# Masked blocks between the halves of a linear attention: one FP32 product instead of three FP32R products, with another order on VectorE

## The chip, the cores and the metric

The kernel runs on one core of a Trainium2 chip. The metric is the device time of one execution in microseconds (us). The program is launched once; the median of three runs before the change is 1372.36 us (1371.91 to 1373.18).

The engines are named as in the profile: PE is TensorE (matmul), PEld its loads of the stationary operand, DVE is VectorE, ACT is ScalarE, POOL is GpSimd, SP is SyncE, which here issues most of the DMA transfers.

## What is computed

Two layers of the same kind, each an attention half A and a mixing half B, on x of 2048 tokens by 512 features, all in float32:

```
x = x + A(layernorm(x));  x = x + B(layernorm(x))      # twice

A: qkv = x @ wqkv, 32 heads of 16
   phi(t) = where(t > 0, t + 1, exp(t)) + 1e-6
   kv[h] = phi(k)[h].T @ v[h];   z[h] = sum over tokens of phi(k)[h]
   o = (phi(q) @ kv) / (phi(q) . z + 1e-6);   A = o @ wo

B: z = gelu(x @ w_in);  z1, z2 = halves of z, z2 layer-normalised
   g = w_sp @ z2 + b_sp;   B = (z1 * g) @ w_out
```

The kernel does not compute v. It uses that kv = phi(k).T @ (x @ wv) can be had from G = x.T @ phi(k), summed over all tokens, since wv.T @ G is the transpose of kv. Of the 512x512 product only the 16x16 blocks on the diagonal belong to a head. The kernel computes the four 128x128 diagonal blocks and multiplies each by a mask that keeps the head blocks. These are the masked blocks. They are then multiplied by wo into W2, so that each query tile needs a single product with W2.

## The kernel before

**Precision.** A matmul here normally runs on FP32R operands, a reduced form of float32. To keep float32 precision, an operand is split into a high part (an ACT copy that rounds to FP32R, `high`, line 105) and a low part (the remainder, a DVE subtraction, `low`, line 108, or on POOL, line 113). `mm3` (lines 117 to 121) makes three matmuls of one product: high x high, high x low, low x high. So every 128-deep step of a product is three matmuls, and every operand costs one ACT and one DVE instruction.

**Buffers.** SBUF is cut into slots: 22 pages of 128x512 (`pg`), 6 quads of 128x2048 (`qd`), 4 bigs (`bg`), 16 larger token tiles (`z`); PSUM into 8 banks. `Slots.get` and `put` hand them out in order of release. A tile that gets a slot waits for the last readers of the slot's former tile. The program is recorded in the order of the calls, with one queue per engine; there is no scheduler, so that the order of the Python statements is the order on each engine.

**First half, `P1.run`** (line 496). Over 16 token tiles of 128, in iterations s = 1 to 17: load, layer norm, transposition through DRAM, the K projection and phi(k), the Q projection and phi(q), and `Gmm`, the accumulation of G into four PSUM banks (12 matmuls per 128 tokens). At the end of every iteration stand side pieces: the weights for later (wv, wo, win2) are loaded into pages by SP (`fetch`) and split into quads or bigs (`piece`). wv takes two quads, high and low, from iterations 1 to 4. The Q projection of the last 6 tiles is put off (`late`, `late_phi`), as PE work that covers the transition.

**`transition`** (line 541) joins the halves:

- z, the sum of phi(k), is split (lines 545, 546) and summed over partitions by a product with ones (555, 556); ACT copies it to `zbc` (559).
- G is copied out of its four banks and split into two quads (550 to 553).
- POOL multiplies phi(q) of a tile with zbc (`a`, line 631).
- `late_phi` finishes a put-off query tile: ACT lines 363 and 364, DVE line 365.
- DVE sums zbc per head into `zeps` (566 to 568); `a2_den` gets the reciprocal of a tile's denominator (643 to 645).
- The masked blocks q = 0 to 3 (572 to 578): each is 4 steps of `mm3`, 12 matmuls of 128x128, 48 in a layer. DVE multiplies each by the mask (577). Then they are split in two pairs (580, 581).
- `a2_mul` (652) applies the denominator to a query tile; for tile 0 an ACT copy (276) puts it in order for four PE transposes (`b`, line 257).
- One put-off Q projection (587), 12 matmuls of 512 columns, stands on PE between the masked blocks and their use.
- W2: four products of a split block with the split wo (592), each split into W2 on ACT and DVE (593); after the second one come the transposes of query tile 0 (596).

**Second half.** `P2.run` takes the query tiles through W2, and goes on to half B; `P4.run` does the token mixing and the output.

Of the kernel before, what the change touches and what calls it, by code (L numbers as in the profile page):

```python
# [11 lines left out]
F32R = mybir.dt.float32r  # L12
AF = mybir.ActivationFunctionType
OP = mybir.AluOpType

P = 128
# [41 lines left out]
def mixer_kernel(ctx: ExitStack, tc: tile.TileContext, x_in, wqkv, wo_d, win1_d, win2_d, wsp_d, bsp_d, wout_d,  # L58
                 ident_d, mask_d, out_d):
    nc = tc.nc  # L60
# [8 lines left out]
    quads = Slots(main, "qd", 6)  # L69
# [34 lines left out]
    def high(h, src):  # L104
        nc.scalar.activation(h, src, AF.Copy)  # L105

    def low(l, src, h):
        nc.vector.tensor_sub(l, src, h.bitcast(F32))  # L108

    def split(h, l, src, pool=False):  # L110
        high(h, src)
        if pool:
            nc.gpsimd.tensor_tensor(l, src, h.bitcast(F32), op=OP.subtract)
        else:
            low(l, src, h)

    def mm3(out, a, b, start, stop):
        (ah, al), (bh, bl) = a, b
        nc.tensor.matmul(out, ah, bh, start=start, stop=False)  # L119
        nc.tensor.matmul(out, ah, bl, start=False, stop=False)  # L120
        nc.tensor.matmul(out, al, bh, start=False, stop=stop)  # L121

    class Weight:


        def __init__(self, slots, shape, pieces, turned=False):
            self.slots, self.shape, self.pieces, self.turned = slots, shape, pieces, turned
            self.h = self.l = None
            self.raw = deque()
            self.n_load = self.n_split = 0  # L130
# [82 lines left out]
    def w_square(src, off, turned=False):  # L213
        return Weight(quads, [P, 4, 512], [src[c * P:(c + 1) * P, off:off + 512] for c in range(4)], turned)

    def w_wo():
        return Weight(bigs, [P, 4, 512], [wo_d[c * P:(c + 1) * P, :] for c in range(4)])
# [4 lines left out]
    def w_in2():  # L222
        return Weight(bigs, [P, 4, FH], [win2_d[f] for f in range(NF)])
# [26 lines left out]
    def feats(ap, turned):  # L250

        return ap.rearrange("p (g c j) -> p c g j" if turned else "p (c g j) -> p c g j", g=4, c=4)
# [48 lines left out]
    class P1:  # L301
        def __init__(self, L):
            self.L = L
            self.st = 2 * L
            self.x, self.ms, self.xT, self.pk, self.kb, self.r, self.xhl = {}, {}, {}, {}, {}, {}, {}
            self.wk, self.wq, self.wv = (w_square(wqkv, 512), w_square(wqkv, 0, True), w_square(wqkv, 1024))
            self.wo, self.win2 = w_wo(), w_in2()
            self.later = deque(range(NT - DEFER, NT))
            self.turn = Turn(f"xt{L}", range(3) if L == 0 else ())
            self.G = None  # L310
            self.zacc = None
# [183 lines left out]

        def run(self):
            side = deque()
            for w in (self.wv, self.wo, self.win2):
                side.extend([w] * len(w.pieces))
            side[0].fetch()  # L500
            ND = NT - DEFER
            for s in range(1, NT + 2):
                self.loadx(s + 3)
                self.turn.load(s + 1)
                turned = 2 <= s < NT and s not in self.turn.by_pe
                if turned:
                    self.T_high(s)
                if s == 1:
                    if not self.kb:
                        self.K(0)  # L510
                    self.K(1)
                elif 2 < s <= NT:
                    self.K(s - 1)
                self.ln_a(s + 2)
                if turned:
                    self.T_low(s)
                if s <= NT:
                    self.K_phi(s - 1)
                if s <= ND:
                    self.Q(s - 1)  # L520
                if s == NT + 1:
                    self.late()
                if s <= NT:
                    self.xsplit(s - 1)
                    self.K_split(s - 1)
                if s + 1 < NT and s + 1 in self.turn.by_pe:
                    self.T(s + 1)
                self.ln_b(s + 2)
                if s <= ND:
                    self.Q_phi(s - 1)  # L530
                if s >= 2:
                    self.Gmm(s - 2)
                if s == NT + 1:
                    self.late_phi()
                for _ in range(min(len(side), 1 if s < 6 else 2)):
                    side.popleft().piece()
                for w in list(side)[:1 if s < 5 else 2]:
                    w.fetch()


    def transition(p1, p2):
        wv, wo = p1.wv, p1.wo
        zh, zl = pages.get(PAGE, F32R), pages.get(PAGE, F32R)
        za = p1.zacc
        nc.vector.tensor_scalar(za, za, NT * PHI_EPS, None, op0=OP.add)
        split(zh, zl, za, True)
        pages.put(za)
        p1.late()
        p1.wk.free()
        g = (quads.get([P, 4, 512], F32R), quads.get([P, 4, 512], F32R))  # L550
        for c in range(4):
            split(g[0][:, c, :], g[1][:, c, :], p1.G[c])
            banks.put(p1.G[c])
        zb = banks.get(PAGE)
        nc.tensor.matmul(zb, ones, zh, start=True, stop=False)
        nc.tensor.matmul(zb, ones, zl, start=False, stop=True)
        pages.put(zh, zl)
        p2.zbc = pages.get(PAGE)
        nc.scalar.activation(feats(p2.zbc, True), feats(zb, False), AF.Copy)
        banks.put(zb)  # L560
        p2.a(0)
        p1.late_phi()
        p2.win1.fetch()
        p2.win1.fetch()
        p2.zeps = small.tile([P, 32], F32, name="zeps", bufs=1)
        nc.vector.tensor_reduce(p2.zeps, p2.zbc.rearrange("p (h d) -> p h d", d=16), axis=mybir.AxisListType.X,
                                op=OP.add)
        nc.vector.tensor_scalar(p2.zeps, p2.zeps, PHI_EPS, PHI_EPS, op0=OP.mult, op1=OP.add)

        p2.a2_den(0)  # L570
        m = pages.get([P, 4, P])
        for q in range(4):
            b = banks.get([P, P])
            s = slice(q * P, (q + 1) * P)
            for c in range(4):
                mm3(b, (wv.h[:, c, s], wv.l[:, c, s]), (g[0][:, c, s], g[1][:, c, s]), c == 0, c == 3)
            nc.vector.tensor_mul(m[:, q, :], b, mask)
            banks.put(b)
        kvh, kvl = pages.get([P, 4, P], F32R), pages.get([P, 4, P], F32R)
        for q in range(0, 4, 2):  # L580
            split(kvh[:, q:q + 2, :], kvl[:, q:q + 2, :], m[:, q:q + 2, :])
        pages.put(m)
        quads.put(*g)
        wv.free()
        p2.a2_mul(0)
        p2.a(1)
        p1.late()
        p2.a2_den(1)
        p2.W2 = (quads.get([P, 4, 512], F32R), quads.get([P, 4, 512], F32R))
        for q in range(4):  # L590
            b = banks.get(PAGE)
            mm3(b, (kvh[:, q, :], kvl[:, q, :]), (wo.h[:, q, :], wo.l[:, q, :]), True, True)
            split(p2.W2[0][:, q, :], p2.W2[1][:, q, :], b)
            banks.put(b)
            if q == 1:
                p2.b(0)
        pages.put(kvh, kvl)
        wo.free()
        p2.a(2)
        p1.late_phi()  # L600
        p2.a2_mul(1)
        p1.late()
        p2.a(3)
        p2.a2_den(2)
        p1.late_phi()
        p2.a2_mul(2)


    class P2:
# [233 lines left out]
        def P1(self, g):  # L843
            self.X[g] = banks.get(PAGE)
            self.product(self.X[g], "P1", g, start=True)
            self.C = self.copied(self.X[g])

        def P2(self, g):
            y = banks.get(PAGE)
            self.product(y, "P2", g, start=True, stop=True)  # L850
            t = self.C
            nc.vector.tensor_add(t, t, y)
            banks.put(y)
            self.gelu_out(2, g, t)
# [762 lines left out]
    p1 = P1(0)  # L1617
    p1.start()
    for L in range(2):
        p1.run()  # L1620
        p2 = P2(p1)
        p2.loadx(0)
        p2.loadx(1)
        transition(p1, p2)
        p2.p4 = p4 = P4(p2, sums)
        p2.run(sums)
        nxt = P1(1) if L == 0 else None
        p4.run(nxt)
        p1 = nxt
# [31 lines left out]
```

## Time and profile before

| | us |
|---|---|
| median of three runs | 1372.36 |
| the profiled execution | 1372.17 |
| its span, from the first to the last instruction | 1370.5 |
| PE busy | 1364.3 |
| DVE busy | 994.8 |
| ACT busy | 620.1 |
| POOL busy | 462.7 |

The span starts at the first instruction; all times in rows of the timeline count from it. A row of the timeline has the start, the busy time, the engine, the line, the operation, the tile written and the tiles read, the shape, and how many instructions are merged in it; in brackets stands how long the engine was idle before it and what ended that. A matmul's busy time is that of the whole pipeline, so consecutive matmuls overlap: their pace is the distance of their starts. A row of the waits names who waited for whom, the total, how often, and the longest. A row of the stretches has the length, then the busy time and the number of instructions of each engine, the granted clock (1.00 is full), the share of the DMA engines and GB/s.

The transition of the first layer lies around 125 to 146 us, that of the second around 809 to 830 us.

### The profile page before, as it was taken

How to read it: one execution, taken by the hardware profiler on the slowest of the kernel's cores; microseconds unless marked ns; L12 is line 12 of the kernel's file. 1: busy time of each engine (PE TensorE's matmuls, PEld its weight loads, DVE VectorE, ACT ScalarE, POOL GpSimd, SP SyncE). 2: the span in 40 equal slices, each digit the busy share in tenths (PEclk: the TensorE clock that was granted, in tenths of full speed). 3: DMA queues.
4: the chain of work that ended last, by engine and by line, in shares of the span. 5: the costliest groups of instructions: out<-in, count | busy, mean ns of one | idle time of the engine just before them, and what ended most of it. 6: DMA issues, size and time to landing. Idle time of an engine off the chain costs nothing.

```text
span 1370.5 us, 18157 instructions
## 1 busy us (share of the span) xinstructions
PE 1364.3 (100%) x6161; PEld 1143.6 (83%) x6161; DVE 994.8 (73%) x1487; ACT 620.1 (45%) x986; POOL 462.7 (34%) x537
## 2 busy tenths in 40 slices
PE   9999999999999999999999999999999999999998
PEld 7888888888888888888888888888888888888887
DVE  7776888666757788887667758877767668995742
ACT  6675544445443443442357745534454452442410
POOL 3343375433233137414113434543230001133450
PEclk9999999999999999999999999999999999999999
DMA  5542377778778988897945413777465579854452
GB/s 178 170 131 62 116 241 254 242 250 290 253 252 282 308 275 278 268 353 232 308 128 155 138 55 119 227 229 244 128 187 205 170 225 326 286 197 163 170 192 91
DMA packets 168957, 287.02 MB, mean 209 GB/s; under 512 B 14624, under 2 KB 58528, under 8 KB 165792
## 3 DMA queue, kind: packets, MB, share of 16 engines
q1 hardware_dynamic: 161808, 254.27, 57.5%
q0 software_dynamic: 5184, 28.31, 5.7%
q10 hardware_dynamic: 1872, 3.28, 0.6%
q8 instruction: 48, 0.79, 0.2%
q14 instruction: 45, 0.37, 0.1%
HBM read 196.94 MB, written 88.87 MB: 209 GB/s over the span
## 4 chain that ended last, share of the span: by engine, by line
PE 100%; DVE 0%; ACT 0%; issue 0%; DVEq 0%
PE bank L121 19%; PE bank L119 19%; PE bank L120 19%; PE bank L1382 10%; PE bank L1381 10%; PE bank L1380 10%; PE bank L1320 3%; PE bank L1322 3%; PE bank L1323 3%; PE bank L833 1%; PE bank L834 1%; PE bank L832 1%; PE bank L257 1%; PE bank L445 0%; PE bank L476 0%; ACT pg L105 0%
## 5 line engine op out<-in xcount | busy, mean ns | idle before, releaser
L1380 PE MATMUL bank<-qd,pg 128*128 128x512 f32 x608 | 236.5, 389 | 0.0
L1381 PE MATMUL bank<-qd,pg 128*128 128x512 f32 x608 | 236.5, 389 | 0.0
L1382 PE MATMUL bank<-qd,pg 128*128 128x512 f32 x608 | 236.5, 389 | 0.0
L1243 DVE TENSOR_TENSOR qd<-qd,qd 128x1024 fp32r<-128x1024 f32 x106 | 150.2, 1417 | 80.0 <-ACT qd L1233 79.3
L1233 ACT ACTIVATE qd<-qd 128x1024 fp32r<-128x1024 f32 x106 | 112.1, 1058 | 136.1 <-DVE qd L1243 49.0
L105 ACT ACTIVATE pg<-pg 128x512 fp32r<-128x512 f32 (+1 forms) x141 | 86.8, 620 | 169.6 <-DVE pg L296 48.7
L121 PE MATMUL bank<-qd,pg 128*128 128x512 f32 x380 | 148.4, 390 | 0.0
L234 POOL TENSOR_SCALAR rs<-mv 128x1 f32<-128x1 f32 x95 | 41.2, 434 | 311.4 <-DVE mv L232 310.9
L1043 POOL TENSOR_TENSOR pg<-pg,pg 128x512 f32<-128x512 f32 x64 | 94.1, 1470 | 138.6 <-DMA pg<-in_wsp_dram 100.4
L1381 PEld LDWEIGHTS bank<-qd,pg 128*128 128x128 f32 x608 | 114.1, 188 | 23.8
L1380 PEld LDWEIGHTS bank<-qd,pg 128*128 128x128 f32 x608 | 114.1, 188 | 23.7
L1382 PEld LDWEIGHTS bank<-qd,pg 128*128 128x128 f32 x608 | 114.1, 188 | 23.6
L1402 POOL TENSOR_TENSOR bg<-bg,pg 128x512 f32<-128x512 f32 x56 | 88.5, 1594 | 125.4 <-DMA pg<-z 120.0
L245 ACT ACTIVATE pg<-pg,nb,rs 128x512 f32<-128x512 f32 x63 | 51.0, 810 | 142.5 <-POOL nb L239 117.7
L108 DVE TENSOR_TENSOR pg<-pg,pg 128x512 fp32r<-128x512 f32 (+1 forms) x139 | 101.6, 733 | 13.4 <-ACT pg L105 6.6
L119 PE MATMUL bank<-qd,pg 128*128 128x512 f32 x284 | 110.7, 390 | 0.0
L120 PE MATMUL bank<-qd,pg 128*128 128x512 f32 x284 | 110.6, 389 | 0.0
L119 PE MATMUL bank<-bg,qd 128*128 128x448 f32 x256 | 94.0, 367 | 0.0
L120 PE MATMUL bank<-bg,qd 128*128 128x448 f32 x256 | 93.6, 366 | 0.0
L121 PE MATMUL bank<-bg,qd 128*128 128x448 f32 x256 | 93.4, 365 | 0.0
L296 DVE STREAM_TRANSPOSE pg<-pg 128x512 f32<-128x512 f32 x79 | 85.3, 1080 | 9.2 <-DMA x<-pg 3.5
L119 PE MATMUL bank<-wo,qd 128*128 128x512 f32 x224 | 87.1, 389 | 0.0
(195 smaller groups left out, 3090.4 us busy)
## 6 DMA issues: line engine op xcount, KB each, us to landing
qd<-s SPq DMA_DIRECT2D x64, 512.0 KB, 4.2
pg<-in_wsp_dram SPq DMA_DIRECT2D x96, 256.0 KB, 4.9
qd<-n POOLq DMA_DIRECT2D x24, 1024.0 KB, 8.7
qd<-in_wsp_dram SPq DMA_DIRECT2D x42, 512.0 KB, 4.3
s<-pg SPq DMA_DIRECT2D x64, 256.0 KB, 4.4
pg<-x SPq DMA_DIRECT2D x64, 256.0 KB, 3.8
n<-pg SPq DMA_DIRECT2D x60, 256.0 KB, 4.4
pg<-z SPq DMA_DIRECT2D x56, 256.0 KB, 4.3
```

Source lines behind the costliest of these rows:

```text
L105: nc.scalar.activation(h, src, AF.Copy)
L108: nc.vector.tensor_sub(l, src, h.bitcast(F32))
L119: nc.tensor.matmul(out, ah, bh, start=start, stop=False)
L120: nc.tensor.matmul(out, ah, bl, start=False, stop=False)
L121: nc.tensor.matmul(out, al, bh, start=False, stop=stop)
L1043: nc.gpsimd.tensor_tensor(t, a, b, op=OP.add)
L1233: nc.scalar.activation(wh, r, AF.Copy)
L1243: nc.vector.tensor_sub(wl, r, wh.bitcast(F32))
L1380: m(out, h[:, o], w[:, 0, j, :], start=start, stop=False, skip_group_check=True)
L1381: m(out, h[:, o], w[:, 1, j, :], start=False, stop=False, skip_group_check=True)
L1382: m(out, l[:, o], w[:, 0, j, :], start=False, stop=stop, skip_group_check=True)
L1402: nc.gpsimd.tensor_tensor(u, u, z1, op=OP.mult)
```

## The change

The products of the masked blocks take the raw float32 weight wv and a raw float32 copy of G, as one FP32 matmul per step (16 in a layer) in place of three FP32R matmuls (48). wv is no longer split: four loads go directly into one quad in iterations 1 to 4 of `P1.run`, where its side pieces stood. The side pieces of wo and win2 stay in their iterations. G gets no low part. On DVE, zeps moves ahead of `late_phi` and the denominator of tile 0 moves between the masks of blocks 1 and 2.

```diff
@@ P1.__init__
-            self.wk, self.wq, self.wv = (w_square(wqkv, 512), w_square(wqkv, 0, True), w_square(wqkv, 1024))
+            self.wk, self.wq = w_square(wqkv, 512), w_square(wqkv, 0, True)
@@ P1.run
-            for w in (self.wv, self.wo, self.win2):
+            for w in (self.wo, self.win2):
                 side.extend([w] * len(w.pieces))
-            side[0].fetch()
+            self.wv = quads.get([P, 4, 512])
...
-                for _ in range(min(len(side), 1 if s < 6 else 2)):
-                    side.popleft().piece()
-                for w in list(side)[:1 if s < 5 else 2]:
-                    w.fetch()
+                if s <= 4:
+                    c = s - 1
+                    nc.sync.dma_start(self.wv[:, c, :], wqkv[c * P:(c + 1) * P, 1024:1536])
+                else:
+                    for _ in range(min(len(side), 1 if s < 6 else 2)):
+                        side.popleft().piece()
+                if s >= 4:
+                    for w in list(side)[:1 if s < 5 else 2]:
+                        w.fetch()
@@ transition
-        g = (quads.get([P, 4, 512], F32R), quads.get([P, 4, 512], F32R))
+        g = quads.get([P, 4, 512])
         for c in range(4):
-            split(g[0][:, c, :], g[1][:, c, :], p1.G[c])
+            nc.scalar.activation(g[:, c, :], p1.G[c], AF.Copy)
             banks.put(p1.G[c])
...
         p2.a(0)
-        p1.late_phi()
-        p2.win1.fetch()
-        p2.win1.fetch()
         p2.zeps = small.tile([P, 32], F32, name="zeps", bufs=1)
         nc.vector.tensor_reduce(p2.zeps, ...)
         nc.vector.tensor_scalar(p2.zeps, ...)
-
-        p2.a2_den(0)
+        p1.late_phi()
+        p2.win1.fetch()
+        p2.win1.fetch()
+
         m = pages.get([P, 4, P])
         for q in range(4):
             b = banks.get([P, P])
             s = slice(q * P, (q + 1) * P)
             for c in range(4):
-                mm3(b, (wv.h[:, c, s], wv.l[:, c, s]), (g[0][:, c, s], g[1][:, c, s]), c == 0, c == 3)
+                nc.tensor.matmul(b, wv[:, c, s], g[:, c, s], start=c == 0, stop=c == 3)
             nc.vector.tensor_mul(m[:, q, :], b, mask)
             banks.put(b)
+            if q == 1:
+                p2.a2_den(0)
...
-        quads.put(*g)
-        wv.free()
+        quads.put(g, wv)
```

## The prediction

> **What bounds the kernel now.** I read the head of the page first: busy times, granted clock, and the chain that ended last.
>
> ```profile
> PE 1364.3 (100%) x6161; PEld 1143.6 (83%) x6161; DVE 994.8 (73%) x1487; ACT 620.1 (45%) x986; POOL 462.7 (34%) x537
> ...
> PEclk9999999999999999999999999999999999999999
> ...
> PE 100%; DVE 0%; ACT 0%; issue 0%; DVEq 0%
> ```
>
> TensorE (PE) fills the span, at the full granted clock, and the chain that ended last is PE alone. Next come the waits of PE, because "100% busy" could still hide some.
>
> ```profile
> PE bank L445 <- DVE pg L440: 2.4, 1, 2.4
> PE bank L476 <- ACT pg L105: 0.2, 1, 0.2
> ```
>
> Both belong to the start of the program. After it PE waits for no engine and no transfer, so a microsecond of PE work taken out is a microsecond won, as long as no new wait appears. The stage that the change touches is read from the stretches (time, then busy time and count of PE, PEld, DVE, ACT, POOL), with the first row for what comes ahead of it, and from the timeline for the borders.
>
> ```profile
> 12.00:100.00 88.00, 88.00 (x392) 72.85 (x391) 68.13 (x113) 63.45 (x109) 32.67 (x50) 1.00 0.47 143
> 129.23:134.54 5.31, 5.31 (x50) 5.31 (x48) 3.50 (x9) 1.72 (x3) 4.44 (x4) 1.00 0.16 52
> 813.01:818.32 5.31, 5.31 (x49) 5.30 (x48) 3.50 (x9) 1.72 (x3) 4.43 (x4) 1.00 0.21 54
> ```
> ```profile
> 129.23 0.23 PE L119 MATMUL bank<-qd,qd 128*128 128x128 f32 x1
> ...
> 134.54 0.44 PE L119 MATMUL bank<-qd,z_h 128*128 128x512 f32 x1
> ...
> 813.01 0.23 PE L119 MATMUL bank<-qd,qd 128*128 128x128 f32 x1
> ...
> 818.32 0.44 PE L119 MATMUL bank<-qd,z_h 128*128 128x512 f32 x1
> ```
>
> From the first masked product to the first matmul of the query projection behind it are 5.31 us, in both layers. Within them the weight loads (PEld) are busy all the time, which they are not in the 88 us ahead (72.85).
>
> **The change, part by part.**
>
> **Taken out: 48 FP32R matmuls of 128x128 per layer.** 5.31 / 48 = 0.111 us each. That is far above a quarter of a 512-column matmul: twelve of those stand between these two rows,
>
> ```profile
> 120.59 0.39 PE L119 MATMUL bank<-qd,z_h 128*128 128x512 f32 x1
> ...
> 123.31 0.39 PE L119 MATMUL bank<-pg,pg 128*128 128x512 f32 x1
> ```
>
> so one takes 2.72 / 12 = 0.227 us, a quarter of it 0.057. At 128 columns the new 128x128 stationary operand of every matmul, not its columns, sets the pace: 0.111 us a load. The change removes 2 x 5.31 = 10.62 us of PE.
>
> **Put in: 16 FP32 matmuls of 128x128 per layer.** No FP32 product stands in this trace. The nearest rows of the same shape and type are the FP32 transposes:
>
> ```profile
> 138.72 0.60 PE L257 MATMUL bank<-ident,pg 128*128 128x128 f32 x4
> 139.07 0.48 PE L119 MATMUL bank<-bg,pg 128*128 128x512 f32 x1
> 139.39 0.39 PE L120 MATMUL bank<-bg,pg 128*128 128x512 f32 x1
> ```
>
> From 138.72 to 139.39 are four transposes and one 512-column matmul: (0.67 - 0.227) / 4 = 0.111 us, again a load each. That is the lower end for a product, 1.78 us per layer. For the upper end I go by the kernel's own arithmetic: three products of high and low parts leave out low x low; a whole product has all four, so at most four loads, 0.443 us, 7.09 us per layer. In between: two parts of each operand stream 4 x 128 = 512 columns, and two stationary parts are two loads, 0.222 us, which fit under the streams. Then it costs what a 512-column matmul costs, 0.227 us, 16 x 0.227 = 3.63 us. I take this one, an estimate: the columns and the loads give nearly the same number, and the trace shows loads hidden under streams everywhere. It saves 5.31 - 3.63 = 1.68 us per layer, 3.36 us in all.
>
> The Trainium skill bears on this. "FP8 and Floating Point Precision", section "TensorE Precision Notes", says that true FP32 takes four passes through the array; by that the lower end falls away and my sum stays. No run here shows it.
>
> **Does what follows keep up?** The blocks go through the mask (VectorE, DVE), are split (ScalarE, ACT; then DVE), and PE reads them at line 592; the transposes of the first query tile come after two of those blocks. The rows of before:
>
> ```profile
> 126.88 1.56 ACT L105 ACTIVATE qd<-bank 128x512 fp32r<-128x512 f32 x3
> ...
> 127.01 2.48 DVE L108 TENSOR_TENSOR qd<-bank,qd 128x512 fp32r<-128x512 f32 x4 [1.18 <-ACT qd L105]
> ...
> 129.43 0.60 ACT L559 ACTIVATE pg<-bank 128x512 f32<-128x512 f32 x1 [0.98 <-PE bank L556]
> ...
> 130.10 5.01 POOL L631 TENSOR_TENSOR pg<-z_q,pg 128x512 f32<-128x512 f32 x4 [2.22 <-ACT pg L559]
> ...
> 130.54 0.63 ACT L364 ACTIVATE z_q<-z_q 128x512 f32<-128x512 f32 x1
> ...
> 131.21 0.69 DVE L365 SCALAR_TENSOR_TENSOR z_q<-bank,z_q 128x512 f32<-128x512 f32 x1 [1.71 <-ACT z_q L364]
> ...
> 131.82 0.68 DVE L566 TENSOR_REDUCE zeps<-pg 128x32 f32<-128x512 f32 x1
> ...
> 132.53 0.18 DVE L568 TENSOR_SCALAR zeps<-zeps 128x32 f32<-128x32 f32 x1
> 132.62 0.68 DVE L643 TENSOR_REDUCE den<-pg 128x32 f32<-128x512 f32 x1
> ...
> 133.33 0.58 DVE L644 TENSOR_TENSOR den<-den,zeps 128x32 f32<-128x32 f32 x1
> ...
> 133.95 0.35 DVE L645 RECIPROCAL den<-den 128x32 f32<-128x32 f32 x1
> ...
> 134.22 0.82 DVE L577 TENSOR_TENSOR pg<-bank,mask 128x128 f32<-128x128 f32 x4
> ...
> 134.67 0.81 ACT L105 ACTIVATE pg<-pg 128x256 fp32r<-128x256 f32 x2 [3.50 <-DVE pg L577]
> ...
> 135.12 0.82 DVE L108 TENSOR_TENSOR pg<-pg,pg 128x256 fp32r<-128x256 f32 x2
> ...
> 135.86 0.68 DVE L652 SCALAR_TENSOR_TENSOR pg<-z_q,den 128x512 f32<-128x512 f32 x1
> ```
> ```profile
> 136.64 0.63 ACT L276 ACTIVATE pg<-pg 128x512 f32<-128x512 f32 x1 [1.15 <-DVE pg L652]
> ...
> 137.35 0.39 PE L119 MATMUL bank<-bg,pg 128*128 128x512 f32 x1
> ```
>
> Before, DVE sat waiting for L364 until 131.21 and then ran without a gap until 136.54. After, the reduction of zeps (L566, L568) goes into that wait: the copy of L559 ends at 130.03, so it runs from 130.1 to about 131.0. L365 still starts at 131.21, as ACT's L363 and L364 are where they were; the 0.2 us left over are lost. Everything behind L365 comes 131.82 to 132.62 = 0.8 us earlier than before. Blocks 0 and 1 are masked at 131.8 to 132.2 (by my price PE makes block 1 at 131.05, two 0.91 us blocks after 129.23), then den, then blocks 2 and 3 by 134.2 (made by 132.86), the low parts to about 135.2, L652 to 135.75, and ACT's copy L276 to 136.5.
>
> PE will be 1.68 us earlier: it reaches line 592 at 135.67 and wants the low parts of blocks 0 and 1, which the masks of 2 and 3 now stand ahead of, but which are done by about 134.65: 1.0 us to spare. Blocks 2 and 3, wanted 1.36 us (six matmuls) later, have theirs by 135.2. The transposes come at 138.72 - 1.68 = 137.04, and L276 ends at 136.5: 0.5 us to spare, where there was 1.45. So I cost the new order at nothing; if DVE ran more than 0.5 us later than I have it, PE would wait for the rest.
>
> This also bounds the gain from the other side. If PE became faster by more than about 2.2 us per layer, it would wait for L276: 138.72 - 136.5. The largest gain is 2 x 2.2 = 4.4 us, whatever an FP32 product costs.
>
> **G without its low part.** Four DVE subtractions (2.48 us from 127.01) go; the four copies on ACT stay. PE's first masked product needs the copies, which end at 128.44, not later than before. What DVE gains here it cannot use, as zeps waits for L559: nothing. Both ends are nothing, since PE starts at 129.23 behind other matmuls.
>
> **The weight raw instead of split.** Four ACT copies and four DVE subtractions per layer go from iterations 1 to 4, and the four loads land in the quad instead of in pages. PE is at 88.00 of 88.00 there, so relief is worth nothing. The loads stay on SyncE's (SP's) queue at the end of the same iterations, except that the first one, formerly ahead of the load of token tile 4, moves behind it and behind a store that waits for ACT; the loads of wo and win2 stand in the same iterations as before. The weight is wanted more than 100 us later. In the second layer the load into the quad waits for its old reader, the last or last but one output tile. Queued behind it on SP are the loads of token tiles and turned tiles; but ahead of it on the same queue stands the store of the last output tile, which waits for the same matmuls. Nothing is added. One quad less each for weight and G only frees buffers earlier.
>
> **Sum.** -3.36 us. The profiled execution took 1372.17 us, 1.67 more than its span of 1370.5, and 0.19 less than the median of 1372.36. Span 1367.1; median 1372.36 - 3.36 = **1369.0**.
>
> **Rivals.** A measurement of this kernel can tell about 0.2% from no change, 2.7 us: faster means below 1369.6, slower above 1375.1.
>
> **Loads half hidden: no change.** If a stationary part can only be loaded while one of the two streams of the part ahead runs, a part costs 0.111 + 0.057 = 0.168 and a product 0.336 us: 16 x 0.336 = 5.38, +0.07 per layer, 1372.5. For it: 128-column matmuls are already bound by loads. Against it: with FP32R and in the transposes a load hides completely. 22 in 100.
>
> **The gain given back: no change.** DVE or ACT arrives late at line 592 or at the transposes, as above; with DVE 0.8 us later than I have it, 0.3 us per layer go, and with it 1.4 us later over half: 1369.6 to 1372. 6 in 100.
>
> **Four loads: slower.** Each of the four part products loads its stationary part anew, at 0.111 us: 0.443 a product, 7.09 us per layer, 1.78 more than now, 1372.36 + 3.56 = 1375.9. It decides from more than three loads a product, 0.333 us, the price of the three matmuls removed. For it: PEld is the busy side of this stretch. Against it: a second load of the same part is needless. 16 in 100. The Trainium skill speaks for a load-bound stage here: "TensorE: Matmul & The Clock Gate", section "Weight-path perf modes — Fast Weight Load (FWL) and DoubleRow", says that the fast weight load is off for FP32, and its section "LDWEIGHTS (loading the stationary operand)" gives columns / 1.2 GHz, 0.107 us for 128; the trace agrees with 0.111. With a load for each of four passes an estimate from that page is 16 x 4 x 0.107 = 6.8 us.
>
> **Not what it says: one pass.** If the hardware took the FP32 operands in one pass, as in the transposes, 1.78 us per layer would do, PE would run into L276, and the gain would stop at 4.4 us: 1368.0. 4 in 100.
>
> **How the numbers follow.** Forecast (two loads under four streams) 52, of which 44 below 1369.6 and 8 within, since 0.2475 us a product would already leave less than 2.7 us; half hidden 22, given back 6, four loads 16 (a seventh of it, 2, within), one pass 4. Faster 48, same 38, slower 14. The range takes in both bounds of the product, 1368.0 and 1375.9, with 0.2 us for the runs: 1367.8 to 1376.1.
>
> **What would show it.** From the first masked product to the query projection 3.6 us instead of 5.31, in both layers; 7.1 or 5.3 would be the rivals. No new row in PE's waits; one that names the mask, the low parts or L276 would show a gain given back. DVE's zeps ahead of its phi at about 130.1, L276's copy over by 136.5. The forecast falls if a product takes over 0.25 us, or if PE waits over 0.3 us in a layer.

## The result, and the profile after

| | before | after |
|---|---|---|
| median of 14 runs each, us | 1373.07 (1371.91 to 1374.48) | 1370.13 (1369.23 to 1372.03) |
| ratio after / before | | 0.9981, 95% interval 0.9973 to 0.9988 |
| the profiled execution, us | 1372.17 | 1371.67 |
| its span, us | 1370.5 | 1370.0 |

The changed kernel is faster by 0.19%: 2.6 us by the ratio, with an interval of 1.6 to 3.7 us, and 2.9 us between the medians. The forecast was 3.4 us, to 1369.0; that figure started from the 1372.36 us of three runs, and the median of 14 is 0.7 us higher. The profiled execution of the changed kernel took 1.5 us more than its median, that of the kernel before 0.9 less. So the two spans differ by only 0.5 us, and the traces have to be compared stage by stage.

The head of the page of the changed kernel, and the waits of PE:

```profile
PE 1362.1 (99%) x6129; PEld 1140.3 (83%) x6129; DVE 985.0 (72%) x1471; ACT 617.0 (45%) x978; POOL 462.9 (34%) x537
```
```profile
PE bank L445 <- DVE pg L440: 2.4, 1, 2.4
PE bank L1327 <- DVE qd L1248: 0.6, 1, 0.6
PE bank L1325 <- ACT pg L105: 0.6, 1, 0.6
PE bank L476 <- ACT pg L105: 0.2, 1, 0.2
```

PE has 32 matmuls fewer than before in the records, and the page shows two waits that were not there: lines 1325 and 1327 are the nested token mixing of the second layer, a thousand microseconds behind the change in the first. They come up again below.

The transition of the first layer, from the timeline of the changed kernel (its line 580 is the masked product):

```profile
129.85 3.73 PE L580 MATMUL bank<-qd,qd 128*128 128x128 f32 x32
...
133.34 0.47 PE L119 MATMUL bank<-qd,z_h 128*128 128x512 f32 x1
133.66 0.39 PE L120 MATMUL bank<-qd,z_h 128*128 128x512 f32 x1
```
```profile
137.06 0.63 ACT L276 ACTIVATE pg<-pg 128x512 f32<-128x512 f32 x1 [1.34 <-DVE pg L657]
...
137.32 0.39 PE L121 MATMUL bank<-bg,pg 128*128 128x512 f32 x1
137.74 0.66 PE L257 MATMUL bank<-ident,pg 128*128 128x128 f32 x4
```

The program has 16 products, the trace has 32 matmuls: the hardware runs each FP32 product as two. From the first one to the query projection are 3.49 us; before they were 5.31. The second matmul of the projection follows the first by 0.32 us, where it was 0.28 before, so 1.78 us are gained by then (5.31 + 0.28 - 3.49 - 0.32).

The last two rows show a loss. At its pace of 0.227 us PE would begin the transposes at 137.55; they begin at 137.74, just after ACT's copy (line 276) ends at 137.69. That is 0.2 us of waiting. The list of waits does not have it, since the busy time of the matmul ahead (0.39 us from 137.32) covers nearly all of it.

The masked blocks start at 129.85 here, and at 129.23 there. Those 0.62 us arise in the first 8 us; a second trace of the kernel before has 0.57 of them as well. They are chance.

Lining up every matmul of a trace with that of the first trace of before gives how far PE is ahead (-) or behind (+) at a place of the program. The kernel before and the changed one were both traced again later, without an edit:

| place (start in the first trace of before, us) | before, second | after, first | after, second | after, third |
|---|---|---|---|---|
| ahead of the masked products (128.9) | +0.57 | +0.63 | +0.62 | +0.35 |
| in the query projection behind them (134.8) | +0.57 | -1.16 | -1.17 | -1.44 |
| at the transposes (138.7) | +0.57 | -0.97 | -1.00 | -1.26 |
| second layer, ahead of the masked products (812.5) | +0.31 | -1.03 | -0.69 | -1.33 |
| in the query projection (818.6) | +0.31 | -2.82 | -2.48 | -3.12 |
| at the transposes (822.5) | +0.31 | -2.63 | -2.31 | -2.93 |
| end (1366.5) | +0.31 | -0.83 | -2.21 | -2.86 |

In each layer 1.79 us are won at the masked blocks, in every trace alike, and 0.17 to 0.19 us lost at the first transpose. At the second transpose another 0.05 to 0.06 us go, so that each transition loses 0.22 to 0.25 us and keeps about 1.55. The first trace of the changed kernel then loses another 1.8 us by its end, most of it at the two late waits; the others lose 0.1.

### The profile page after: what moved, and what is told of

Same layout as the page of the kernel before. It is cut to its first block, busy times and chain, and to the rows that moved or that the text cites. A ratio compares the mean times of both kernels' runs of the same rounds, so it can differ in the third digit from the quotient of the medians.

```text
span 1370.0 us, 18070 instructions
## 1 busy us (share of the span) xinstructions
PE 1362.1 (99%) x6129; PEld 1140.3 (83%) x6129; DVE 985.0 (72%) x1471; ACT 617.0 (45%) x978; POOL 462.9 (34%) x537
## 4 chain that ended last, share of the span: by engine, by line
PE 96%; DMA 2%; DVE 1%; issue 1%; ACT 0%; DVEq 0%; ACTq 0%; POOLq 0%; SPq 0%
PE bank L121 19%; PE bank L119 19%; PE bank L120 19%; PE bank L1385 10%; PE bank L1387 10%; PE bank L1386 10%; PE bank L1327 2%; PE bank L1328 2%; PE bank L1325 2%; DMA qd<-in_wsp_dram 1%; PE bank L838 1%; PE bank L839 1%; PE bank L837 1%; PE bank L257 1%; PE bank L580 1%
## 5 line engine op out<-in xcount | busy, mean ns | idle before, releaser
L1248 DVE TENSOR_TENSOR qd<-qd,qd 128x1024 fp32r<-128x1024 f32 x106 | 143.8, 1357 | 83.4 <-ACT qd L1238 82.8
```

The source lines that it names most:

```text
L1248: nc.vector.tensor_sub(wl, r, wh.bitcast(F32))
```

## The experiments

### The order on VectorE

**FP32 products with the old order.** Everything of the change but the order of zeps, phi and the denominator.

```diff
@@ after, transition
+        p1.late_phi(); p2.win1.fetch(); p2.win1.fetch()
         p2.zeps = ...
-        p1.late_phi(); p2.win1.fetch(); p2.win1.fetch()
+        p2.a2_den(0)
...
-            if q == 1:
-                p2.a2_den(0)
```

> The FP32 products and the raw weight and G stay; the order on VectorE is that of before: phi of the put-off tile, then zeps, then the denominator of tile 0, then the four masks. Theory: PE takes 3.5 us for the masked products as after the change (5.3 before), and the old order gives part of it back: masks, low parts and the copy of query tile 0 come 0.6 to 0.8 us later than in the changed kernel, so PE waits 0.6 to 1.0 us in each layer at line 592's products or at the transposes instead of 0.2, and the time lies 0.8 to 1.6 us above the changed kernel, 1.2 to 2.2 below the kernel before. Rival: the order is worth nothing, the time is that of the changed kernel within 0.3 us and PE's wait at the transposes stays at 0.2 us. Rival: the order is the whole gain, the time is that of the kernel before.

Measured: 1370.94 us, median of 11 runs, beside 1370.30 for the changed kernel (11 runs) and 1372.87 for the kernel before (27 runs) on the same chip; ratio to before 0.9985 (0.9976 to 0.9994). The difference of 0.64 us to the changed kernel lies inside the scatter of the runs, and it is less than the 0.8 expected. The trace is finer. Of the waits of PE the one at the transposes (there is a late one too, of 0.4 us on a transfer at line 1324), and the transition:

```profile
PE bank L257 <- ACT pg L276: 0.5, 2, 0.2
```
```profile
129.12 3.73 PE L581 MATMUL bank<-qd,qd 128*128 128x128 f32 x32
...
136.52 0.63 ACT L276 ACTIVATE pg<-pg 128x512 f32<-128x512 f32 x1 [1.15 <-DVE pg L656]
...
137.21 0.66 PE L257 MATMUL bank<-ident,pg 128*128 128x128 f32 x4 [0.23 <-ACT pg L276]
```

From the first masked product to ACT's copy are 136.52 - 129.12 = 7.40 us; in the changed kernel 137.06 - 129.85 = 7.21. The new order brings the copy 0.19 us earlier, not 0.8, and PE loses 0.39 us at the first transpose in each layer, where the changed kernel loses 0.19 and 0.6 to 1.0 were expected (lined-up traces; the 1.79 us at the masked blocks are the same). The order is worth 0.2 us a layer.

**The new order alone.** Three FP32R matmuls and the splits as before.

```diff
@@ before, transition
-        p1.late_phi(); p2.win1.fetch(); p2.win1.fetch()
         p2.zeps = ...
-        p2.a2_den(0)
+        p1.late_phi(); p2.win1.fetch(); p2.win1.fetch()
...
             banks.put(b)
+            if q == 1:
+                p2.a2_den(0)
```

> Three FP32R matmuls per step and the split weight and G as before; only the order on VectorE is the new one. Theory: PE needs 5.31 us for the masked blocks and has no wait in the transition either way, so the time is that of the kernel before within 0.5 us. Rival: the order by itself brings part of the gain: 1 us or more below the kernel before.

Measured: 1372.70 us (11 runs) beside 1372.87, ratio 0.9998 (0.9989 to 1.0007). No gain: with 5.31 us of masked products nobody waits for VectorE in either order. The gain is that of the product.

### What an FP32 product costs

At 128 columns each of the 32 matmuls takes 3.49 / 32 = 0.109 us, and two explanations give this number: a load of the stationary part (0.111), or twice 128 columns (a quarter of 0.227 each, 0.113 together). Two runs tell them apart.

**512 columns.** The product takes all of G; the mask reads the same block.

```diff
-            b = banks.get([P, P])
+            b = banks.get(PAGE)
...
-                nc.tensor.matmul(b, wv[:, c, s], g[:, c, s], start=c == 0, stop=c == 3)
-            nc.vector.tensor_mul(m[:, q, :], b, mask)
+                nc.tensor.matmul(b, wv[:, c, s], g[:, c, :], start=c == 0, stop=c == 3)
+            nc.vector.tensor_mul(m[:, q, :], b[:, s], mask)
```

> Each FP32 product takes all 512 columns of G in place of the 128 that are used; the mask reads the same diagonal block. What sets the price of an FP32 product? Theory: the trace shows two matmuls per product, and each streams its columns twice: at 512 columns a half takes 0.43 to 0.46 us, a product 0.87 to 0.91, the masked blocks 14 to 14.6 us per layer in place of 3.5, and the time rises by 21 to 22 us. Rival: each half streams its columns once and at 128 columns the loads of the weights set the pace: a half 0.227 us, the masked blocks 7.3 us per layer, the time up by 7.6 us.

**64 columns.** Two products of 64 columns in place of one of 128.

```diff
+            for j in range(2):
+                o = slice(j * 64, (j + 1) * 64)
+                t = slice(q * P + j * 64, q * P + (j + 1) * 64)
                 for c in range(4):
-                    nc.tensor.matmul(b, wv[:, c, s], g[:, c, s], start=c == 0, stop=c == 3)
+                    nc.tensor.matmul(b[:, o], wv[:, c, s], g[:, c, t], start=c == 0, stop=c == 3)
```

> Each FP32 product is made as two of 64 columns, 32 products per layer with the same result. Theory: a load of the stationary part takes 0.111 us whatever streams, so two halves of 64 columns cost as much as two of 128, and the masked blocks take 7.0 us per layer in place of 3.5; the time rises by 6.5 to 7.5 us. Rival: the streams alone set the price and the loads are free: 3.5 us per layer, the time stays.

The stretch from the first masked product to the query projection in the three kernels: changed kernel, 512 columns, 64 columns. Columns: length, then busy time and count of PE, PEld, DVE, ACT, POOL.

```profile
129.85:133.34 3.49, 3.49 (x33) 3.48 (x32) 2.62 (x6) 1.99 (x4) 2.61 (x3) 1.00 0.30 75
```
```profile
129.87:143.20 13.33, 13.33 (x33) 5.91 (x32) 3.93 (x9) 2.13 (x4) 4.95 (x4) 1.00 0.08 21
```
```profile
129.89:136.96 7.07, 7.07 (x66) 7.07 (x64) 4.75 (x9) 2.13 (x4) 4.96 (x4) 1.00 0.15 39
```

At 512 columns the starts of the 32 halves lie 0.43 us apart. The stretch gives a little less, 13.33 / 32 = 0.417 us, because the projection's first matmul is recorded early and its second follows late:

```profile
143.20 0.79 PE L119 MATMUL bank<-qd,z_h 128*128 128x512 f32 x1
143.83 0.39 PE L120 MATMUL bank<-qd,z_h 128*128 128x512 f32 x1
```

With the second one it comes to 143.83 - 129.87 - 0.227 = 13.73 us for 32, which is 0.43 each. That is near two streams of 512 columns (2 x 0.227), far from one, and the loads are busy for less than half of the stretch. The time rose to 1391.05 us, by 20.9, a little less than expected. At 64 columns a half takes 7.07 / 64 = 0.110 us, with the loads busy throughout, although it streams half as much: here the columns do not set the pace, and the busy loads say that the load does. The time rose to 1376.87, by 6.7 (one run each, against the changed kernel's 1370.13). So an FP32 product is two loads, each with a stream that takes as long as its columns twice, and at 128 columns both come to the same 0.11 us. Whether the columns pass twice or once at half the pace, these times do not tell. Four loads a product (the records have two) and loads half hidden (0.168 us a half) are excluded.

By the Trainium skill, page "FP8 and Floating Point Precision", section "TensorE Precision Notes", true FP32 makes four passes. The measurement agrees as far as it goes: two matmuls, each with the time of two streams.

### What the split of the weight was worth

```diff
                     nc.sync.dma_start(self.wv[:, c, :], wqkv[c * P:(c + 1) * P, 1024:1536])
+                    if s > 1:
+                        h, l = pages.get(PAGE, F32R), pages.get(PAGE, F32R)
+                        split(h, l, self.wv[:, c - 1, :])
+                        pages.put(h, l)
```

> As the changed kernel, but three of the four splits of the raw weight (a ScalarE copy and a VectorE subtraction each) stay in iterations 2 to 4, into pages that nothing reads. Theory: PE is full there and hides them; the time is that of the changed kernel within 0.4 us. Rival: the relief of ScalarE and VectorE in the first half is part of the gain: 0.7 us or more above the changed kernel.

Measured: 1369.92 us (11 runs) beside 1372.75 for the kernel before on that chip; ratio 0.9978 (0.9969 to 0.9986). The changed kernel, on other chips, has 0.9981 and 0.9983. Three ACT copies and three DVE subtractions per layer put back cost nothing that can be seen, and PE is full in that stage: in the lined-up trace it loses 0.02 us between 14 and 129 us, as it does in the changed kernel. As forecast, the relief in the first half is worth nothing.

### Why ACT's copy came late

The prediction had ACT's copy of query tile 0 over 7.3 us after the first masked product; it was over after 7.84. The rows of VectorE and GpSimd in the changed kernel:

```profile
130.73 2.51 POOL L636 TENSOR_TENSOR pg<-z_q,pg 128x512 f32<-128x512 f32 x2 [2.23 <-ACT pg L564]
```
```profile
131.40 0.64 DVE L570 TENSOR_SCALAR zeps<-zeps 128x32 f32<-128x32 f32 x1
...
133.66 0.87 DVE L649 TENSOR_TENSOR den<-den,zeps 128x32 f32<-128x32 f32 x1
...
135.18 1.19 DVE L108 TENSOR_TENSOR pg<-pg,pg 128x256 fp32r<-128x256 f32 x2
```
```profile
133.19 2.56 POOL L636 TENSOR_TENSOR pg<-z_q,pg 128x512 f32<-128x512 f32 x2
```

The four GpSimd products end at 132.01, 133.24, 134.49 and 135.75. L570 takes 0.64 us, where the same operation took 0.18 before (L568); it ends at 132.04. L649 ends at 134.53, and the first subtraction of line 108 takes 0.85 us and ends at 136.03. The first two end within 0.05 us of the end of a GpSimd instruction, and the third 0.28 us after one, less than its own 0.42. The reductions and the masks between them have their usual length. The same offsets stand in the trace of before, where subtractions of line 108 meet a GpSimd product: four of 256 elements end 0.28 to 0.29 us after it, ten of 512 elements 0.55 us. To see whether GpSimd is the cause, its products of tiles 1 to 3 were held back behind the last split:

```diff
         p2.a2_mul(0)
+        hold = small.tile([P, 1], F32, name="hold", bufs=1)
+        nc.gpsimd.tensor_copy(hold, kvl[:, 3, 0:1].bitcast(F32))
         p2.a(1)
```

> As the changed kernel, but a GpSimd copy of one column of the last low part stands ahead of the products of query tiles 1 to 3 with zbc, so that these start about 5 us later, after VectorE has split the masked blocks. Theory: in the changed kernel three VectorE instructions of the transition wait for the end of a GpSimd instruction: the add to the denominator takes 0.87 us (0.19 alone), the first low part 0.85 (0.42 alone). With GpSimd quiet they take 0.19 and 0.42, the masks of blocks 2 and 3 come 0.7 us earlier, ScalarE's copy of query tile 0 ends 0.8 to 1.1 us earlier against the first masked product, and the 0.2 us at the transposes is gone in both layers. Behind it the denominators of tiles 1 and 2 come later and PE may wait at the first product with W2. Rival: the lateness comes from the new order on VectorE itself; the durations and the wait of 0.2 us stay.

VectorE and ACT of that kernel, whose first masked product starts at 129.47:

```profile
131.02 0.64 DVE L570 TENSOR_SCALAR zeps<-zeps 128x32 f32<-128x32 f32 x1
...
133.28 0.19 DVE L651 TENSOR_TENSOR den<-den,zeps 128x32 f32<-128x32 f32 x1
...
134.12 0.99 DVE L108 TENSOR_TENSOR pg<-pg,pg 128x256 fp32r<-128x256 f32 x2
```
```profile
135.81 0.63 ACT L276 ACTIVATE pg<-pg 128x512 f32<-128x512 f32 x1 [1.15 <-POOL hold L592]
```

L651 is the former L649: 0.19 instead of 0.87. The two subtractions of line 108 together take 0.99 instead of 1.19, the first of them 0.42. L570, which meets the one product that was not moved, keeps its 0.64. ACT's copy starts 135.81 - 129.47 = 6.34 us after the first masked product, 0.87 earlier than in the changed kernel, and PE loses nothing at the transposes. (The row names GpSimd's copy as what ended ACT's wait, but ACT starts 0.09 us after VectorE's line 659 ends, as it does behind line 657 of the changed kernel.) So the lateness is VectorE waiting for GpSimd, and not the order as such. As a kernel it is no better: one run of 1371.70 us, since the products held back now delay the denominators, PE loses 0.4 us in each layer at later transposes, and late waits came up as well: 0.6 us at line 1327 in the second layer, and one on a transfer in the first.

The Trainium skill describes this: "SBUF — State Buffer", section "SBUF: two separate sides", says that VectorE and GpSimd share a port pair as an exclusive lock, taken for the whole instruction, by a VectorE operation with two SBUF inputs or in a two-port mode. The trace agrees: L649 and line 108 read two SBUF operands, the masks read one from PSUM, and the reductions have one operand in all; L570 has a single SBUF operand, so that by the page it would be in a two-port mode, which no run here shows. The same section of the Trainium skill gives the lock to whichever starts first; the late wait further down is recorded the other way round.

### The transposes one W2 product later

```diff
-            if q == 1:
+            if q == 2:
                 p2.b(0)
```

> As the changed kernel, but the transposes of query tile 0 stand after the third W2 product on PE instead of the second, 0.68 us later. Theory: the wait of 0.2 us at the transposes is gone in both layers and nothing else is late, so PE gains 0.4 us: 0.2 to 0.6 us below the changed kernel. Rival: the wait moves on to the first product with W2, or the low parts of query tile 0 are late there, and the time stays or rises by 0.2 to 0.5 us.

Measured: 1369.85 us (11 runs), 1372.75 before on that chip; ratio 0.9979 (0.9970 to 0.9988). The loss at the transposes is gone: in the lined-up traces PE comes out of each transition 1.8 us ahead of where it went in, instead of 1.55. That is the size expected, but in the times it does not stand clear of the changed kernel, nor of the 1369.92 us of the run above, which has the transposes in their old place. By its trace it is the best order seen here in the transitions; elsewhere that trace has two late waits, 0.6 us at line 1325 and 0.7 at line 1386.

### The late waits: belonging to the change, or chance?

> The changed kernel once more, for its trace. Theory: masked blocks 3.5 us and 0.2 us of waiting at the transposes in both layers, as in the first trace; the two waits of 0.6 us late in the second layer and the 0.6 us at the start are chance and are gone or elsewhere, so the span is 1367.5 to 1369. Rival: the two late waits belong to the changed kernel, they stand again at the same steps, and the span is 1370 again.

> The kernel before once more, for its trace. Theory: late waits of PE of half a microsecond are chance and occur here too in some executions; the span is 1370.5 to 1372.5, and what it has over 1370.5 are such waits. Rival: PE never waits after the start in this kernel, and a longer span comes from somewhere else.

> The changed kernel a third time, for its trace. Theory: masked blocks 3.5 us, the loss of 0.2 us at the transposes in both layers as twice before; late waits of PE of half a microsecond stand at other steps or not at all, so that the span is 1367.5 to 1370. Rival: waits at the same two steps as in the first trace, span 1370.

Measured: the changed kernel 1370.30 us (11 runs), span of the trace 1368.6; its third trace 1367.9 (one run, 1369.64). Neither has a late wait at line 1325 or 1327 of the second layer's end. The second trace lost 0.4 us at line 1325 in the first layer instead, to a transfer. The kernel before once more: 1372.49 us, span 1370.8, no wait after the start, so that its trace does not bear out that such waits occur there. Its times scatter as widely, though (1371.91 to 1374.48 before, 1369.23 to 1372.03 after).

The wait at line 1327, around 1180 us, stands in the first trace of the changed kernel alone; its cause stays open. Where the one at line 1325 comes from can be read from VectorE, GpSimd and ACT around 1193 us. Kernel before, then the changed kernel in its first trace:

```profile
1192.70 0.68 DVE L108 TENSOR_TENSOR pg<-pg,pg 128x512 fp32r<-128x512 f32 x1
1192.98 0.53 POOL L1186 DMA_DIRECT2D qd<-n  x1 [2.19 <-PE bank L1323]
...
1193.42 2.04 DVE L1300 TENSOR_TENSOR pg<-z_z,z_z 128x256 f32<-128x256 f32 x2
1193.53 1.30 POOL L1400 TENSOR_TENSOR bg<-bg 128x512 f32<-128x512 f32 x1
...
1195.55 0.63 ACT L105 ACTIVATE pg<-pg 128x512 fp32r<-128x512 f32 x1 [3.24 <-DVE pg L1300]
```
```profile
1191.41 0.53 POOL L1191 DMA_DIRECT2D qd<-n  x1 [2.19 <-PE bank L1328]
1191.62 2.20 DVE L108 TENSOR_TENSOR pg<-pg,pg 128x512 fp32r<-128x512 f32 x1
1191.95 1.30 POOL L1405 TENSOR_TENSOR bg<-bg 128x512 f32<-128x512 f32 x1
...
1193.85 0.76 DVE L1305 TENSOR_TENSOR pg<-z_z,z_z 128x256 f32<-128x256 f32 x2
...
1194.70 0.63 ACT L105 ACTIVATE pg<-pg 128x512 fp32r<-128x512 f32 x1 [3.48 <-DVE pg L1305]
...
1197.12 0.47 PE L1325 MATMUL bank<-qd,pg 128*128 128x512 f32 x1 [0.57 <-ACT pg L105]
```

In both kernels one GpSimd product of 1.30 us holds up VectorE there. PE waits for ACT's copies, and the first of these waits for two differences (line 1300, in the changed kernel 1305) that VectorE makes behind the low part (line 108). In the kernel before the product holds up the first difference; the two are over 0.63 us after the product, and the last of ACT's copies ends at 1197.93, just before PE goes on at 1197.97. In this trace VectorE ran half a microsecond late against PE, and the product holds up the low part: 2.20 us instead of 0.68. The differences still stand behind it and are over only 1.35 us after the product, and PE loses 0.74. The low part ends 0.56 us after the product, as the held-up ones of its length do elsewhere, so this looks like the same lock, although by the record the low part started 0.33 us ahead of the product. In the twelve traces 17 VectorE instructions with two SBUF operands are held up by a product that is recorded as starting behind them, and each time GpSimd was issuing a transfer when they began (here line 1191, 1191.41 to 1191.94); whether that is the reason was not tested.

Of nine traces with the FP32 products (three of the changed kernel, six of variants) four have this wait, and in exactly these four the product holds up that low part; of three with the FP32R products none has it, and in all three it holds up the difference. Whether the change makes the wait more likely stays open: the traces are too few, and no run here forces it.

## Why the prediction was right

**The price of the product** was the step on which it hung, and its mechanism was right: two loads, and streams as long as four of the product's columns. The estimate was 0.227 us, measured are 0.218. The gain per layer is 1.79 us, where 1.68 were forecast. One pass (0.111), four loads (0.443) and loads half hidden (0.336) are refuted by these 0.218 us and the two loads a product in the records. That the number came so near is partly luck of the shape: at 128 columns loads and streams cost the same, so that either limit alone would have given it; the runs with 512 and 64 columns show both.

**Where PE starts and stops** held: the masked products start right behind the product with ones, and nothing is seen to change with G's missing low part and the raw weight; for the weight a run shows it, for G only the start of the masked products.

**The order, costed at nothing, was the step that failed in size.** The prediction gave VectorE 0.8 us of lead and PE 0.5 us to spare at the transposes. It took the durations of VectorE from the trace of before, where they had met GpSimd's instructions at other moments. Moved by 0.8 us, zeps and the first low part now meet one, and the denominator, which met one before, waits longer. Of the 0.8 us 0.2 were left, the spare 0.5 became a loss of 0.25 us per layer, not far from the 0.3 at which the forecast itself would have fallen. The rival "the gain given back" thus came true with a small part of its price.

**The sum.** Twice (1.79 - 0.25) gives 3.1 us, against 3.36 forecast: the product gave a little more, and the order took a little more. Measured are 2.6 (1.6 to 3.7). The rest can be the waits of 0.7 us late in the second layer, present in some traces and absent in others; that they account for it was not shown. The gain is clear of zero, but it lies on the border (2.7 us) that the prediction drew between "faster", which it gave 48 in 100, and "same", which it gave 38.

**Two other sources of the gain**, raised for the experiments, are refuted: the order alone gives 0.9998, the relief of the first half nothing.

## What to carry to other kernels

Three FP32R products on split operands beat one FP32 product while columns set the pace (at 512 columns 3 x 0.227 us against 2 x 0.43); where the operand is so narrow that loads do (three loads of 0.111 us against two), a raw FP32 product is cheaper, and it saves the splits. When instructions are moved on VectorE, their durations in the old trace include what they waited for on GpSimd: look at what GpSimd runs at the new place. In a kernel where PE never waits, the gain is read from lined-up traces stage by stage, because waits of 0.7 us elsewhere, present in some executions only, are a quarter of the effect.

## What the runs showed of the hardware

An FP32 matmul instruction of the program appears as two matmuls with a load each in the records, and each takes 0.110 us at 64 columns, 0.109 at 128 and 0.43 at 512, where an FP32R matmul takes 0.111 at 128 and 0.227 at 512. A VectorE instruction with two SBUF operands that a GpSimd product holds up ends after that product, by 0.05 us with 32 elements, 0.28 with 256 and 0.55 with 512: 0.19 us became 0.87, 0.42 became 0.85, and 0.68 became 2.20, the last through a product that is recorded as starting 0.33 us after it.
